# Gated complex recurrence and a maxout feed-forward block on one core: another order of all steps, with fewer changes of the array's tile shape

## The chip, the core and the metric

The kernel runs on one NeuronCore of a Trainium2 chip. The metric is the device time of one execution in microseconds (us). A profiled execution gives a span, which runs from the first to the last recorded instruction; the device time holds some more around it.

## The reference, cut to what matters

```python
# B, H, S, D = 4, 8, 768, 48; all float32
mag = np.sqrt(a_re * a_re + a_im * a_im)
scale = np.minimum(mag, 0.999) / (mag + 1e-06)
a_re_n, a_im_n = (a_re * scale, a_im * scale)
for t in range(S):                      # complex state S_re, S_im of D x D for each batch and head
    ar, ai = (a_re_n[:, :, t, :, None], a_im_n[:, :, t, :, None])
    new_re = ar * S_re - ai * S_im
    new_im = ar * S_im + ai * S_re
    kv = np.einsum('bhd,bhe->bhde', k[:, :, t], v[:, :, t])
    S_re, S_im = (new_re + kv, new_im)
    y[:, :, t] = np.einsum('bhd,bhde->bhe', q[:, :, t], S_re)
x = y.transpose(0, 2, 1, 3).reshape(B * S, H * D)          # 3072 x 384
h = np.maximum(np.maximum(x @ w1, x @ w2), x @ w3)         # weights 384 x 768
out = h @ w_out                                            # 768 x 384
```

The four weights of the feed-forward block lie in DRAM as 64-bit floats; the kernel makes 32-bit floats of them itself.

## The kernel before

The 3072 tokens are worked in 12 groups of two tiles x and y of 128 tokens each (two batches, the same 128 positions). A step is a word such as `Ay:4`: step A of tile y of group 4. A long text, `SCHEDULE`, lists all steps of all groups; the kernel runs through it once and emits the instructions of each step as it comes to it. Nothing reorders them afterwards: each engine's proxy ties every instruction to the one before it on the same engine,

```python
                if self.last is not None:
                    tc.add_manual_dep(ins.ins, self.last.ins.name, order, reason="the schedule's order")
```

so the text fixes the order on TensorE (PE), VectorE (DVE), ScalarE (ACT), GpSimd (POOL) and the DMA queues of SP and POOL. Waits between engines come from the data and from the buffers.

Two more lists go with it. `SLOTS` has one digit for each PSUM tile that a step takes, in order: `tag="ps" + next(slots)`, four rooms 0, 2, 4 and 6 of two banks each, so it says which earlier result has to be read before a step may write. `OTHER` names the steps that run on their second engine (DVE in place of ACT, or DVE in place of an accumulating DMA of POOL; for `Zf`, `Zg` POOL in place of DVE).

The steps, by the names that come back below:

- Weights. Twelve blocks of w1, w2, w3 and w_out. `WL` loads a block raw on SP's queue into a room that is free at that time (a part of the weights' own store, the activations' buffer `xhx`, or `strassen`, the buffer of later sums); `Wb`, `Wc`, `We` (DVE, 128x768 elements) and `Wa` (ACT) convert it. `Wg` adds one block into another by a DMA of POOL (or on DVE). `T`, `t`, `M`, `m` make a product of w1 and w_out, `wp`, used by the first group; `J1` to `J4` make differences of w_out for the later groups.
- Gates. `Lr`, `Li` load a_re and a_im; `sqr`, `sqi`, `add`, `lnL`, `expe`, `expw`, `lne`, `relu`, `Lnop`, `abs`, `addw`, `pw`, `lnw`, `expL`, `mulai`, `mulw`, `stt`, `xor`, `half`, `atan`, `turn` turn them into the logarithm of the magnitude (`Ln`) and the angle (`w`), on ACT and DVE; for group 0 the steps are done for each half alone (`sqr0`, `sqr1` and so on).
- Angles. `cs` (PE) cumulates the angles, `t`, `nf`, `af`, `sa`, `sb` make sine and cosine. `Cd` carries the last angle into the next group by a small DMA of POOL.
- Attention by chunks of 64 positions. `sums` (PE) cumulates `Ln`; `En`, `Ek`, `Eq` are its exponentials; `mk`, `mq`, `uk`, `uq`, `kEn` scale k and q; `tpk`, `tpq` (PE) transpose them, `Kc`, `Qc` bring them to SBUF; `F` (PE) and `f0` to `f3` (ACT) make the decay factors at the boundaries of sub-chunks, `Q1`, `Q2`, `KB`, `QB`, `QG` apply them; `A` and `B` (PE) are the scores, `g0` to `g3` (DVE) and `b0`, `b1` (ACT) pick their valid parts into `atm`; `dk` (PE) and `h0` to `h3` advance the state; `y` (PE) is the output of the tile, the step `x` (`xx`, `xy`) copies it for the feed-forward part.
- Feed-forward. For group 0, tile by tile: `U01x` to `U22y` are the products with w1, w2, w3 (PE), `u..` the maxima (DVE, ACT), `O` the product with w_out, `o` its copy. For groups 1 to 11, with both tiles at once: `U01`, `U02`, `U11`, `U12` and the maxima; then the output product in the seven products `P1` to `P7` of a Strassen scheme (PE, four matmuls each), beside `Px` and `Py`, with the sums `S1` to `S4` ahead of them and `r1`, `r6`, `r75`, `r57`, `ox`, `oy` behind them on DVE (`r1` on ACT). `Dx`, `Dy` store a tile's 192 KB on SP's queue.

The order interleaves the feed-forward products of one group with the attention of the next one and the gates of the one after it.

A matmul's tile shape is the part of the 128x128 array that it uses. `U`, `O`, `P`, `Px`, `Py`, `T`, `M`, `pw` use all rows and columns; `F`, `sums`, `dk` use 64x64 quarters; `A`, `B`, `y` use 32 columns, four of them side by side; `tp` 64 rows, `cs` 64 columns. A stay, below, is a stretch of PE's list that keeps one shape. `A` is 64 small matmuls each with a weight load of its own, `B` 32, `y` 112, `dk` 64, `tp` 32, `F` and `sums` 16 each (each list a little shorter for the first chunk of a sequence), while `U` is 18 large ones, `P` four, `O` nine.

All instructions are recorded under one line, L201, since one helper emits them; they are told apart by the names of their tiles.

Of the kernel before, what the change touches and what calls it, by code (L numbers as in the profile page):

```python
# [26 lines left out]
turn1:0 nfx:0 Wc9:0 afx:0 Wa10:0 T2:0 sqr:1 sqi:1 sax:0 sbx:0 t2:0 Wc10:0 We9:0 add:1 ukx:0 WL11:0 Lvx:0 uqx:0 We10:0
csy:0 tpkx:0 tpqx:0 lnL:1 ty:0 Kcx:0 Eqy:0 expw:1 kEnx:0 xor:1 nfy:0 Lky:0 Liy:2 Lix:2 WL1:0 WL2:0 Lrx:2 WL4:0 Lvy:0
Lry:2 dkx:0 Fy:0 Wb11:0 relu:1 Qcx:0 expe:1 QBx:0 Q2x:0 mqy:0 abs:1 Wa11:0 Wc11:0 Wb1:0 half:1 lne:1 f2y:0 Eny:0 f1y:0
Eky:0 f3y:0 h1x:0 f0y:0 pw:1 Wa1:0 lnw:1 expL:1 We11:0 Wb2:0 Q1x:0 h2x:0 Wc1:0 h3x:0 QGx:0 Wa2:0 afy:0 say:0 mulai:1  # L30
We1:0 CL:0 Wb4:0 Wc2:0 mulw:1 We2:0 M0:0 M1:0 Zg:0 Lnop:1 Cdx:0 Wg1:0 Cdy:0 Wa4:0 sby:0 sqr:2 sqi:2 sumsx:1 Ax:0 M2:0
Wg2:0 stt:1 Wc4:0 mky:0 atan:1 uqy:0 Ekx:1 Eqx:1 Enx:1 We4:0 add:2 lnL:2 expe:2 relu:2 g0x:0 g1x:0 uky:0 KBx:0 g2x:0
g3x:0 turn:1 m1:0 Bx:0 b0x:0 tpqy:0 tpky:0 m0:0 b1x:0 Kcy:0 WL5:0 Lkx:1 csx:1 csy:1 tx:1 yx:0 xor:2 Qcy:0 Wb5:0 nfx:1
Q2y:0 Q1y:0 ty:1 expw:2 afx:1 Wa5:0 xx:0 abs:2 Ay:0 sax:1 QBy:0 Wc5:0 KBy:0 We5:0 addw:2 kEny:0 nfy:1 g0y:0 g1y:0 g2y:0
g3y:0 Wg4:0 Z4:0 Wg5:0 half:2 Cdx:1 Z3:0 WL7:0 WL8:0 Lqx:1 Lqy:1 Lky:1 U11x:0 sumsy:1 dky:0 By:0 lnw:2 Wb7:0 QGy:0
u11x:0 expL:2 mulai:2 mulw:2 Eny:1 Eky:1 Eqy:1 b0y:0 Wa7:0 h1y:0 b1y:0 afy:1 U02x:0 U01x:0 yy:0 u01x:0 xy:0 sbx:1 say:1
sby:1 h2y:0 Wc7:0 Cdy:1 Z2:0 Lvx:1 h3y:0 stt:2 U12x:0 Liy:3 atan:2 lne:2 We7:0 u12x:0 mkx:1 mqx:1 u02x:0 ukx:1 turn:2
mky:1 uqx:1 Wb8:0 U01y:0 U02y:0 U11y:0 u11y:0 u01y:0 U12y:0 Wa8:0 u02y:0 u12y:0 uky:1 csx:2 tx:2 nfx:2 tpkx:1 tpqx:1
tpky:1 Lnop:2 Wc8:0 We8:0 Wg7:0 Kcx:1 Kcy:1 Qcx:1 U21y:0 Fx:1 sumsx:2 Fy:1 Lix:4 f3x:1 f1x:1 f2x:1 f0x:1 f3y:1 f1y:1
f2y:1 f0y:1 u21y:0 csy:2 kEnx:1 Q1x:1 Wg8:0 ty:2 Eqx:2 Ekx:2 U21x:0 u21x:0 Enx:2 mqy:1 uqy:1 Q2x:1 nfy:2 U22y:0 dkx:1  # L40
tpqy:1 Qcy:1 afy:2 say:2 h0x:1 h1x:1 QBx:1 Ax:1 g0x:1 u22y:0 KBx:1 g1x:1 Lqx:2 Lky:2 Lvy:1 Lkx:2 Lix:3 h0y:1 mqx:2 h2x:1
Q2y:1 h3x:1 Q1y:1 g2x:1 g3x:1 sbx:2 sqi:3 sby:2 afx:2 Oy:0 Fx:2 oy:0 sax:2 Bx:1 b1x:1 b0x:1 Ay:1 QGx:1 yx:1 Lvx:2 Lrx:3
Lry:3 Lqy:2 U22x:0 kEny:1 QBy:1 g0y:1 g1y:1 g2y:1 KBy:1 g3y:1 f2x:2 f3x:2 xx:1 sqr:3 sumsy:2 Eqy:2 f0x:2 f1x:2 add:3
u22x:0 dky:1 By:1 Ox:0 J3:0 mkx:2 h1y:1 b1y:1 Eny:2 Eky:2 lnL:3 expe:3 b0y:1 relu:3 h2y:1 ukx:2 mky:2 uqx:2 xor:3 uky:2
QGy:1 expw:3 ox:0 abs:3 tpkx:2 tpqx:2 kEnx:2 h3y:1 yy:1 Kcx:2 Qcx:2 xy:1 dkx:2 Fy:2 addw:3 mqy:2 Q2x:2 half:3 QBx:2
f1y:2 f0y:2 f3y:2 lne:3 lnw:3 expL:3 f2y:2 uqy:2 h0x:2 KBx:2 Q1x:2 U11:1 u11:1 mulw:3 h1x:2 J1:0 Lnop:3 tpky:2 tpqy:2
kEny:2 Ax:2 Kcy:2 Qcy:2 Lrx:4 Lry:4 Lvx:3 Liy:4 Dx:0 Lvy:2 U01:1 Q1y:2 g0x:2 g1x:2 g2x:2 Q2y:2 g3x:2 mulai:3 h2x:2 h3x:2
Cdy:2 Cdx:2 sumsy:3 Bx:2 u01:1 Ay:2 Fx:3 KBy:2 g0y:2 g1y:2 h0y:2 b0x:2 b1x:2 Eny:3 g2y:2 stt:3 Eqy:3 sqr:4 atan:3 g3y:2
U02:1 U12:1 QGx:2 QBy:2 J2:0 turn:3 sqi:4 f1x:3 f0x:3 f2x:3 f3x:3 add:4 yx:2 u12:1 u02:1 csx:3 csy:3 lnL:4 xx:2 tx:3
xor:4 S1:1 nfx:3 dky:2 sumsx:3 ty:3 nfy:3 h1y:2 Eky:3 expe:4 Enx:3 Eqx:3 expw:4 S2:1 QGy:2 h2y:2 h3y:2 relu:4 afx:3 S3:1  # L50
By:2 Ekx:3 P5:1 P6:1 P1:1 P7:1 sax:3 sbx:3 Lqy:3 Lqx:3 abs:4 mqx:3 afy:3 b0y:2 b1y:2 say:3 r1:1 sby:3 addw:4 lne:4 Lix:5
Dy:0 Lry:5 Lkx:3 Lvx:4 Px:1 P2:1 S4:1 mkx:3 P3:1 Py:1 J4:0 yy:2 xy:2 r6:1 r75:1 uqx:3 ukx:3 Lky:3 mqy:3 uqy:3 r57:1
mky:3 tpkx:3 tpqy:3 tpqx:3 Lrx:5 Lvy:3 Liy:5 h0x:3 Kcx:3 kEnx:3 P4:1 Qcy:3 lnw:4 Qcx:3 uky:3 dkx:3 Fy:3 U11:2 f1y:3
expL:4 f0y:3 Lnop:4 oy:1 Q2x:3 half:4 mulai:4 mulw:4 f3y:3 f2y:3 h1x:3 QBx:3 Q1x:3 ox:1 stt:4 h0y:3 sqi:5 h2x:3 Q1y:3
Cdx:3 Cdy:3 h3x:3 Dy:1 Dx:1 atan:4 sqr:5 add:5 lnL:5 turn:4 Lix:6 Lqy:4 Lry:6 Lrx:6 Lky:4 Lqx:4 U01:2 u01:2 u11:2 U02:2
tpky:3 Kcy:3 csy:4 expe:5 ty:4 relu:5 xor:5 u02:2 S3:2 QGx:3 csx:4 tx:4 expw:5 abs:5 Ax:3 nfy:4 nfx:4 KBx:3 kEny:3 g0x:3
g1x:3 afx:4 U12:2 u12:2 g2x:3 g3x:3 S1:2 Fx:4 f2x:4 f3x:4 f1x:4 f0x:4 sumsy:4 Eny:4 Eqy:4 Eky:4 Lkx:4 dky:3 Lvy:4 Liy:6
sumsx:4 Bx:3 Ekx:4 Eqx:4 S2:2 Q2y:3 mqy:4 h1y:3 addw:5 sby:4 sbx:4 sax:4 b1x:3 b0x:3 h0x:4 h2y:3 KBy:3 h3y:3 mky:4 QBy:3
mkx:4 ukx:4 P7:2 P6:2 P5:2 P1:2 yx:3 Ay:3 xx:3 lnw:5 lne:5 expL:5 r1:2 Enx:4 Px:2 Py:2 P4:2 QGy:3 S4:2 r6:2 g0y:3 g1y:3
g2y:3 g3y:3 afy:4 mulw:5 r75:2 half:5 P2:2 By:3 P3:2 b1y:3 b0y:3 yy:3 say:4 xy:3 r57:2 mqx:4 uqx:4 ox:2 mulai:5 tpqx:4  # L60
tpkx:4 oy:2 kEnx:4 Fy:4 uky:4 Lnop:5 Kcx:4 uqy:4 sumsx:5 U11:3 KBx:4 Lqx:5 Cdx:4 f2y:4 stt:5 f3y:4 Ekx:5 f0y:4 Lkx:5
Dy:2 Dx:2 Qcx:4 Enx:5 Q1x:4 Cdy:4 u11:3 Eqx:5 QBx:4 mkx:5 QGx:4 U01:3 atan:5 Q2x:4 u01:3 f1y:4 h0y:4 U02:3 u02:3 sqr:6
dkx:4 h1x:4 sqi:6 h2x:4 h3x:4 Fx:5 f0x:5 f3x:5 add:6 f1x:5 f2x:5 Ax:4 g0x:4 Lqy:5 g1x:4 Bx:4 lnL:6 expe:6 g2x:4 g3x:4
U12:3 lne:6 b1x:4 tpky:4 turn:5 mqx:5 b0x:4 tpqy:4 Qcy:4 u12:3 kEny:4 S1:3 csy:5 ty:5 csx:5 Kcy:4 dky:4 nfy:5 S3:3
sumsy:5 h1y:4 h2y:4 tx:5 nfx:5 h3y:4 afy:5 yx:4 Eky:5 Eny:5 Eqy:5 afx:5 Q2y:4 Q1y:4 sbx:5 P5:3 P1:3 P7:3 Lky:5 sax:5
# [1 line left out]
Py:3 r1:3 By:4 P2:3 P4:3 say:5 sby:5 QGy:4 g1y:4 abs:6 g2y:4 g3y:4 b1y:4 b0y:4 KBx:5 mqy:5 r6:3 r75:3 r57:3 kEnx:5 oy:3
Q1x:5 uky:5 xor:6 Lry:7 sqr:7 Fy:5 f2y:5 sumsx:6 uqy:5 f3y:5 yy:4 P3:3 ox:3 f0y:5 Lkx:6 xy:4 QGx:5 addw:6 U11:4 Liy:7
Dx:3 QBx:5 Ekx:6 mkx:6 Enx:6 Lvx:5 f1y:5 lnw:6 Lqx:6 h0y:5 u11:4 Q2x:5 expL:6 mulai:6 mulw:6 U01:4 u01:4 tpky:5 h0x:5
Eqx:6 Kcy:5 tpqy:5 stt:6 Ax:5 Lix:7 atan:6 g0x:5 Qcy:5 g1x:5 g2x:5 Bx:5 kEny:5 g3x:5 b0x:5 Q2y:5 U02:4 sqi:7 b1x:5 add:7  # L70
lnL:7 relu:7 expe:7 u02:4 U12:4 Fx:6 f2x:6 S3:4 f3x:6 half:6 turn:6 f0x:6 u12:4 Lvy:5 dky:5 h1y:5 Q1y:5 f1x:6 sumsy:6
dkx:5 Eny:6 csy:6 csx:6 h1x:5 mqx:6 S1:4 Dy:3 ty:6 nfy:6 S2:4 Eqy:6 Lqy:6 mqy:6 Eky:6 P1:4 KBy:5 tx:6 nfx:6 afx:6 lne:7
expw:7 afy:6 P7:4 abs:7 Lky:6 Ay:5 QBy:5 g0y:5 g1y:5 g2y:5 yx:5 g3y:5 addw:7 sbx:6 sax:6 ukx:6 uqx:6 By:5 say:6 P5:4
xx:5 P6:4 r1:4 r6:4 lnw:7 xor:7 S4:4 half:7 Px:4 P2:4 b0y:5 Py:4 r75:4 P4:4 r57:4 P3:4 expL:7 mulw:7 QGy:5 oy:4 tpqx:6
tpkx:6 b1y:5 Lnop:7 mky:6 Qcx:6 Q1x:6 ox:4 Liy:8 kEnx:6 yy:5 sumsx:7 xy:5 Cdx:6 Enx:7 Fy:6 f2y:6 f0y:6 f3y:6 mulai:7
f1y:6 Eqx:7 QBx:6 QGx:6 Q2x:6 stt:7 Lqx:7 Ekx:7 Lix:8 U01:5 sqi:8 Lry:8 Cdy:6 Kcx:6 Lrx:8 Lvx:6 dkx:6 h1x:6 sby:6 mqx:7
# [966 lines left out]
```

## Time and profile before

| | |
|---|---|
| device time, median of 3 runs | 558.63 us (558.34 to 559.18) |
| profiled execution, span | 553.2 us, 22687 instructions |
| PE matmuls busy | 523.6 us (95%), x10086 |
| PE weight loads busy | 448.1 us (81%), x10086 |
| DVE busy | 482.1 us (87%), x752 |
| ACT busy | 368.2 us (67%), x653, of which 49 table loads 62.9 us |
| POOL busy | 70.8 us (13%), x113 |
| DMA | 47.51 MB, mean 86 GB/s |

For the profiled execution only the span is listed, no device time of its own; the difference between the median and the span is 5.4 us. PE's busy time counts from the start of a matmul to its modelled end, and weight loads (PEld) run beside it. In the rows of the profile, `A<-Q,K 112*32 112x80` means that tile A is written from Q and K, the stationary tile takes 112 rows and 32 columns of the array, and the moving one is 112x80; `x64` is the number of instructions in the row, and a bracket behind a row gives the idle time of the engine ahead of it and what ended it. "issue" stands for idle time in which the engine waited for nothing that the profile shows. Queue q8 carries instructions that are fetched.

### The profile page before, as it was taken

To read this page: it belongs to the slowest core of one execution; us is meant where nothing else is said; L and a number is where in the kernel's file an instruction comes from. 1 tells how busy PE (TensorE), PEld (TensorE's weight loads), DVE (VectorE), ACT (ScalarE), POOL (GpSimd) and SP (SyncE) were. 2 spreads that over 40 slices of the span, in tenths; PEclk is the share of its full clock that TensorE was granted. 3 is DMA by queue.
4 is the path that set the end of the run, shared out by engine and by line. 5 is a ranking of instruction groups with operands and counts; after the bars stand their busy time and mean duration, and the time that the engine had idled before them with its cause. 6 is when DMAs were issued, how large, how long until landed. Compare 5 with 4: busy or idle time off the path is not lost.

```text
span 553.2 us, 22687 instructions
## 1 busy us (share of the span) xinstructions
PE 523.6 (95%) x10086; PEld 448.1 (81%) x10086; DVE 482.1 (87%) x752; ACT 368.2 (67%) x653; POOL 70.8 (13%) x113
## 2 busy tenths in 40 slices
...
GB/s 203 295 246 176 174 131 79 50 128 63 109 38 124 67 68 51 61 44 88 72 121 58 35 85 108 101 91 54 62 125 20 32 105 72 2 31 2 31 1 28
DMA packets 141953, 47.51 MB, mean 86 GB/s; under 512 B 130464, under 2 KB 135584, under 8 KB 141856
## 3 DMA queue, kind: packets, MB, share of 16 engines
...
q8 instruction: 79, 1.29, 1.0%
q14 instruction: 18, 0.15, 0.1%
...
## 4 chain that ended last, share of the span: by engine, by line
PE 84%; DVE 7%; ACT 4%; SPq 2%; issue 1%; DMA 1%; DVEq 0%; ACTq 0%
PE up L201 33%; PE op L201 24%; PE y L201 7%; PE A L201 5%; PE tp L201 4%; PE dk L201 3%; PE sums L201 2%; PE cs L201 2%; DVE w L201 2%; SPq L201 2%; PE F L201 2%; PE B L201 1%; DMA wo<-in_moe_w_dram 1%; DVE atm L201 1%; ACT f L201 1%
## 5 line engine op out<-in xcount | busy, mean ns | idle before, releaser
L201 PE MATMUL up<-xhx,w 128*128 128x256 f32 x792 | 177.0, 382 | 0.1
L201 PEld LDWEIGHTS up<-xhx,w 128*128 128x128 f32 x792 | 148.6, 190 | 21.5 <-PE B L201 0.3
L201 ACT ACT_TABLE_LOAD x49 | 62.9, 1283 | 1.6 <-PEq L1027 0.8
L201 ACT COPY atm<-B 32x128 f32<-32x128 f32 x96 | 24.6, 256 | 37.8 <-DVE atm L201 19.7
L201 PE MATMUL op<-wo,xhx 128*128 128x192 f32 (+1 forms) x220 | 48.4, 363 | 0.0
L201 DVE TENSOR_TENSOR Q<-Q,f 112x1024 f32<-112x1024 f32 (+1 forms) x48 | 45.4, 952 | 1.7 <-ACT Q L201 1.2
L201 POOL DMA_DIRECT2D ar<-nf x40 | 34.6, 1305 | 60.3 <-DVE ar L201 48.9
L201 ACT ACTIVATE f<-F 48x232 f32<-48x232 f32 x96 | 34.5, 359 | 10.1 <-PE F L201 6.1
L201 PEld LDWEIGHTS op<-wo,xhx 128*128 128x128 f32 x220 | 36.5, 190 | 4.6 <-issue 0.6
L201 PE MATMUL y<-atm,vb 128*32 128x64 f32 x1152 | 39.0, 221 | 0.2 <-ACT K L201 0.2
L201 PE MATMUL y<-QG,g 112*32 112x64 f32 x1408 | 38.0, 219 | 0.2 <-issue 0.2
L201 PEld LDWEIGHTS y<-atm,vb 128*32 128x32 f32 x1152 | 32.4, 109 | 5.3 <-issue 2.9
L201 PEld LDWEIGHTS y<-QG,g 112*32 112x32 f32 x1408 | 34.8, 109 | 0.3 <-issue 0.3
L201 DVE TENSOR_TENSOR ot<-ot,op 128x384 f32<-128x384 f32 (+1 forms) x56 | 25.6, 464 | 10.7 <-PE op L201 6.4
L201 PE MATMUL op<-wo,strassen 128*128 128x192 f32 x176 | 33.0, 331 | 0.0
L201 POOL DMA_DIRECT2D Ln<-e x9 | 8.3, 923 | 192.2 <-ACT e L201 53.8
L201 PE MATMUL A<-Q,K 112*32 112x80 f32 x1536 | 31.6, 234 | 1.4 <-DVE Q L201 1.4
L201 DVE COPY_PREDICATED atm<-masko,A 128x256 f32<-128x256 uint8 x72 | 31.2, 435 | 1.7
L201 PE MATMUL op<-w,strassen 128*128 128x192 f32 x176 | 32.2, 329 | 0.0
L201 PEld LDWEIGHTS A<-Q,K 112*32 112x32 f32 x1536 | 27.3, 110 | 4.2 <-issue 3.1
L201 PEld LDWEIGHTS op<-wo,strassen 128*128 128x128 f32 x176 | 28.8, 190 | 0.8
L201 ACT COPY Q<-tp 112x1024 f32<-112x1024 f32 x22 | 22.3, 1014 | 10.7 <-PE tp L201 10.5
...
## 6 DMA issues: line engine op xcount, KB each, us to landing
ar<-in_a_re_dram SPq DMA_DIRECT2D x24, 192.0 KB, 3.1
ai<-in_a_im_dram SPq DMA_DIRECT2D x24, 192.0 KB, 3.5
...
out_dram<-ot SPq DMA_DIRECT2D x23, 192.0 KB, 2.6
...
```

The source lines that it names most:

```text
L201: ins = f(*a, **kw)
```

## The change

The three lists are replaced: the order of all steps, the PSUM rooms and the choice of engines. The work is the same. PE's list has 167 stays in place of 190. Weight blocks are loaded and converted in another order at the start, and steps of equal or like shape stand together more often: two `U` or all `P` steps in a row, `tpk` beside `tpq`, and `A`, `y`, `B` beside each other. The order of group 4 to 11 around some of the places, old list above and new list below (parts of lines):

```
-Ay:4 xx:4 KBy:4 ukx:5 uqx:5 Lrx:7 tpqx:5 S2:3 expw:6 relu:6 QBy:4 Lnop:6 mky:5 tpkx:5 S4:3 Kcx:5 g0y:4 Qcx:5 P6:3 Px:3
-Py:3 r1:3 By:4 P2:3 P4:3 say:5 sby:5 QGy:4 ...
+expL:6 sbx:5 Q1y:4 h1x:4 P1:3 P7:3 h1y:4 Q2y:4 h2x:4 QBy:4 h3x:4 h2y:4 S1:3 h3y:4 Ay:4 g0y:4 yx:4 By:4 afx:5 g1y:4
+xx:4 sax:5 g2y:4 S2:3 g3y:4 b1y:4 sqr:7 P5:3 Py:3 P4:3 Px:3 P6:3 S4:3 b0y:4 r1:3 QGy:4 mqx:5 mulai:6 mulw:6 uqx:5 r6:3
...
+Lnop:7 tpqx:6 QBy:5 Ay:5 g0y:5 g1y:5 afy:6 g2y:5 Qcx:6 Q1x:6 g3y:5 lnw:7 yx:5 xx:5 By:5 b0y:5 QBx:6 b1y:5 P2:4 QGy:5
...
+Liy:10 h2x:7 h3x:7 lnw:9 r6:6 r75:6 r57:6 b1y:7 QGy:7 xx:7 sumsx:8 dky:7 h1y:7 Fx:8 yy:7 S4:6 Enx:8 Ekx:8 expL:9 h2y:7
...
+dkx:10 h1x:10 dky:10 Fx:11 Ekx:11 h2x:10 h3x:10 f0x:11 f3x:11 f1x:11 f2x:11 afx:11 sumsy:11 Eky:11 Eqy:11 Eny:11
+h1y:10 KBy:10 h2y:10 Ay:10 g0y:10 Lkx:11 Lqx:11 h3y:10 yx:10 By:10 mqy:11 g1y:10 g2y:10 Px:9 P2:9 Lky:11 g3y:10 S1:9
...
-dkx:11 u02:10 S3:10 Ax:11 Dy:9 g0x:11 Q1y:11 h0x:11 h1x:11 h1y:11 U12:10 u12:10 Ay:11 S1:10 g0y:11 g1y:11 g1x:11 Bx:11
+Q1y:11 h1x:11 Q2y:11 QGx:11 KBy:11 U12:10 u11:10 QBy:11 u12:10 S1:10 P1:10 P7:10 Ay:11 yx:11 By:11 g0y:11 S2:10 g1y:11
```

The head and the end:

```
-Lrx:0 sqr0:0 Lix:0 sqi0:0 add0:0 lnL0:0 expe0:0 expw0:0 lne0:0 relu0:0 WL0:0 Wb0:0 Liy:0 Wa0:0 sqi1:0 Zf:0 Lry:0 sqr1:0
-WL3:0 Lqy:0 Lry:1 WL6:0 WL9:0 Lkx:0 Lix:1 WL10:0 Lqx:0 Lrx:1 Liy:1 Lnop0:0 abs0:0 Fx:0 pw0:0 sumsx:0 add1:0 xor0:0
+Lix:0 sqi0:0 Lrx:0 xor0:0 Zf:0 sqr0:0 add0:0 CL:0 Zg:0 Liy:0 sqi1:0 lnL0:0 expe0:0 expw0:0 lne0:0 relu0:0 Lry:0 sqr1:0
+xor1:0 Lnop0:0 add1:0 abs0:0 pw0:0 WL0:0 Wb0:0 lnL1:0 sumsx:0 half0:0 expe1:0 expw1:0 relu1:0 lne1:0 Lnop1:0 WL3:0
...
+dkx:0 h1x:0 afx:1 Ekx:1 QBx:0 Wc4:0 half:2 We4:0 Wg4:0 Ay:0 Bx:0 b1x:0 b0x:0 yx:0 Lkx:1 Eqx:1 g0y:0 Enx:1 lnw:2 h2x:0
...
+h1y:0 b0y:0 WL7:0 Wc5:0 U01x:0 u01x:0 stt:2 U11x:0 atan:2 Lky:1 Wb7:0 yy:0 xy:0 h2y:0 We5:0 turn:2 Z2:0 Wa7:0 sby:1
...
-u01:11 U11:11 U02:11 u11:11 u12:11 P1:11 S3:11 Dy:10 u02:11 S1:11 S2:11 Px:11 P2:11 P5:11 S4:11 P6:11 r1:11 r6:11 Py:11
-P3:11 P7:11 r75:11 ox:11 P4:11 Dx:11 r57:11 oy:11 Dy:11
+u02:11 U11:11 U12:11 u11:11 u12:11 Px:11 P3:10 S1:11 S3:11 P6:10 Dy:9 r6:10 P5:11 P7:11 r75:10 S2:11 P6:11 Py:11 P4:11
+P1:11 r57:10 S4:11 P3:11 oy:10 ox:10 Dx:10 r1:11 Dy:10 r6:11 r75:11 r57:11 P2:11 ox:11 Dx:11 oy:11 Dy:11
```

Three small edits of the code go with the lists: step `t` of the angles and step `r1` may run on DVE where `OTHER` names them, and `P2` and `P3` may come in either order.

```diff
-            activation(out=T["t", x], in_=T["cs", x], func=AF.Copy, scale=-1.0, bias=MAGIC)
+            if other():
+                dve.tensor_scalar(out=T["t", x], in0=T["cs", x], scalar1=-1.0, scalar2=MAGIC, op0=OP.mult, op1=OP.add)
+            else:
+                activation(out=T["t", x], in_=T["cs", x], func=AF.Copy, scale=-1.0, bias=MAGIC)
...
+            last = i not in (2, 3) or ("half", g) in T
+            if i in (2, 3):
+                T["half", g] = i
             for n in range(4):
                 mm(out=r[i], lhsT=left[:, n], rhs=factor(i)[:, (n + 2 * (g % 2)) % 4],
-                   start=i in (1, 5, 6, 7) and n == 0, stop=i != 2 and n == 3)
+                   start=i in (1, 5, 6, 7) and n == 0, stop=last and n == 3)
...
             if name == "r1":
-                act.copy(out=xl, in_=r[1])
+                copy(out=xl, in_=r[1])
```

The new `OTHER` names `tx:5`, `ty:5`, `ty:9`, `ty:10` and `r1:1`, `r1:4` among its steps.

More of the change, by code (lines that the diff above doesn't have):

```diff
@@ L27 @@
[L27 to L65, printed above, removed]
-Ay:4 xx:4 KBy:4 ukx:5 uqx:5 Lrx:7 tpqx:5 S2:3 expw:6 relu:6 QBy:4 Lnop:6 mky:5 tpkx:5 S4:3 Kcx:5 g0y:4 Qcx:5 P6:3 Px:3
@@ L67 @@
[L67 to L76, printed above, removed]
```

143 lines of the change are left out of this document (93 added, 50 removed).

## The prediction

> **What bounds the kernel now.** I read the page's first lines, then a table of busy time by stretch, the chain of waits, and last the time line of PE's weight loads. The page says that PE is the fullest engine and heads the chain that ended last; its 20172 records of matmuls and weight loads come to the 1.29 MB that queue q8 fetched, at 64 bytes each, in 79 blocks.
>
> ```profile
> span 553.2 us, 22687 instructions
> PE 523.6 (95%) x10086; PEld 448.1 (81%) x10086; DVE 482.1 (87%) x752; ACT 368.2 (67%) x653; POOL 70.8 (13%) x113
> q8 instruction: 79, 1.29, 1.0%
> PE 84%; DVE 7%; ACT 4%; SPq 2%; issue 1%; DMA 1%; DVEq 0%; ACTq 0%
> 0.00:20.00 20.00, 9.33 (x75) 4.81 (x76) 11.92 (x26) 16.04 (x35) 15.01 (x49) 1.00 0.92 239
> 20.00:91.70 71.70, 58.28 (x1110) 46.40 (x1112) 70.75 (x113) 65.99 (x111) 16.56 (x17) 0.95 0.80 178
> 91.70:140.00 48.30, 47.99 (x1096) 38.15 (x1087) 46.84 (x72) 35.88 (x65) 4.22 (x5) 1.00 0.42 82
> 140.00:549.60 409.60, 408.01 (x7824) 358.79 (x7818) 351.93 (x543) 250.28 (x444) 35.07 (x42) 1.00 0.32 63
> ```
>
> The columns of the stretches are length, then busy time of PE, PEld, DVE, ACT, POOL. Two regimes are to be seen. Up to 91.7 us, where PE starts step O of the first tile, DVE is busy 82.7 us: 8.1 us of its idle time lie in the first 20 us, 1.0 behind them. PE idles 24.1 us there. So DVE's list, converting weights beside the first attention tiles, sets when PE gets to that place. From 91.7 on PE is busy 456.0 of 457.9 us, and the end is PE's remaining work. Busy PE is not PE at its pace, so gaps inside its steps have to be looked for separately.
>
> The span is 553.2 us and the runs' median 558.63; 5.4 us lie outside the span, and I carry that over.
>
> **The price of a change of shape.** A stay of PE in one shape costs a fixed amount beside its matmuls, which shows where two equal steps stand together instead of apart (pieces of the chain: start, length, step, records):
>
> ```profile
> 122.76 4.08 PE up L201 x18
> 129.68 7.97 PE up L201 x36
> 385.59 1.50 PE op L201 x8
> 399.74 2.80 PE op L201 x16
> 396.90 1.04 PE tp L201 x32
> 485.65 1.93 PE tp L201 x64
> 397.94 0.81 PE sums L201 x16
> 449.45 1.46 PE sums L201 x32
> 98.52 0.46 PE L201 MATMUL B<-QB,KB 112*32 112x32 f32 x32
> 98.80 1.33 PE L201 MATMUL A<-Q,K 112*32 112x80 f32 x64
> 341.88 0.46 PE L201 MATMUL B<-QB,KB 112*32 112x32 f32 x32
> 342.27 1.14 PE L201 MATMUL dk<-vb,uk 64*64 64x48 f32 x64
> ```
>
> Twice 4.08 less 7.97 is 0.19 us for a stay in the full shape (0.20 from op), 0.15 for tp, 0.16 for the 64x64 steps. For the 32-column steps A, B and y, B hands over after 0.28 us to its own shape and after 0.39 to another: 0.11, and I take 0.13 with an allowance for the way in, which no row parts. [...]
>
> Counted on the two lists, 190 stays become 167. Behind step O 156 become 140: 9 fewer of 32 columns, 4 of 64x64, 4 of tp, one more of the full array. That is 9 x 0.13 + 4 x 0.16 + 4 x 0.15 - 0.19 = **-2.2 us** (-1.9 to -2.6). The 7 fewer ahead of it fall where PE waits for DVE, and count nothing.
>
> **DVE's list up to step O.** Taking each instruction at the pace of its group, it holds 83.3 us against 83.4: no difference. The added choices (t and r1 may go to DVE: 4 and 2 times, about 0.5 us each) are paid for by others of the step list going back to ACT, and ACT's two more table loads come behind step O, where ACT is idle 172 of the 457.9 us of the last two stretches. **0.**
>
> **The head.** DVE's idle time of the first 20 us decides, since nothing gives it back before step O:
>
> ```profile
> 5.45 0.56 DVE L201 CUSTOM_DVE_ANT_0 L<-L,e 128x384 f32<-128x384 f32 x1 [2.50 <-ACT L L201]
> 8.20 0.87 DVE L201 TENSOR_SCALAR xhx<-w 128x768 f32<-128x768 f32 x1 [2.19 <-DMA w<-in_moe_w_dram]
> 10.80 0.56 DVE L201 CUSTOM_DVE_ANT_0 L<-L,e 128x384 f32<-128x384 f32 x1 [1.14 <-ACT e L201]
> 14.30 0.61 DVE L201 SCALAR_TENSOR_TENSOR Ln<-L,e 128x384 f32<-128x384 f32 x1
> 17.05 0.63 DVE L201 TENSOR_SCALAR xhx<-wo 128x768 f32<-128x768 f32 x1 [1.01 <-DMA wo<-in_moe_w_dram]
> ```
>
> The new list loads the four 192 KB pieces of a ahead of weight block 0, which moves from third to fifth. At the 239 GB/s of the first stretch its 0.77 MB then end about 1.6 us later than the 8.2 us of this row. Lnop0 stays at about 9.0; the second half's chain of five ACT steps (0.42 us apart) brings Lnop1 to about 12.6 instead of 14.3, but with only Wb0 and half0 to fill the time DVE idles some 1.6 us before it, then 0.7 at mqx (it waits for PE's cold sums), and 0.3 twice. My hand chain puts DVE's idle time at 9.1 to 9.6 against 8.1 to 8.7: **+1.0 us** (0 to +2).
>
> **The tail.** PE now waits 1.2 us before its last step, P4, for DVE's ox, and DVE then has 0.6 us to do:
>
> ```profile
> 548.01 1.57 PE L201 MATMUL op<-w,xhx 128*128 128x192 f32 x8 [1.23 <-DVE ot L201]
> 549.61 0.62 DVE L201 TENSOR_TENSOR ot<-ot,op 128x192 f32<-128x192 f32 x2 [1.40 <-PE op L201]
> out_dram<-ot SPq DMA_DIRECT2D x23, 192.0 KB, 2.6
> ```
>
> In the new list the last step is P2, and on the built program it has no wait on DVE; ox then comes behind it, 0.46 us by its pace. With the gap seen in PE's starts (1.4 us) that is **-0.9 us** (-1.4 to 0). What could be late next is r1, which must wait for the store Dx of the group before; between P6 of that group and P1 PE has 7 us of steps, and the chain of DVE steps and the store (3.3 + 2.6 us by its median) fits.
>
> **The instruction fetches.** This is the term that decides. Inside steps, with no wait in the program, PE stops:
>
> ```profile
> 100.21 0.11 PEld L201 LDWEIGHTS y<-atm,vb 128*32 128x32 f32 x1
> 100.67 0.11 PEld L201 LDWEIGHTS y<-QG,g 112*32 112x32 f32 x1 [0.35 <-issue]
> 104.79 0.33 PEld L201 LDWEIGHTS dk<-vb,uk 64*48 64x48 f32 x18 [0.25 <-issue]
> 100.66:104.78 4.12, 3.99 (x128) 3.60 (x127) 4.05 (x9) 2.86 (x6) 0.00 (x0) 1.00 0.51 92
> 196.56 0.33 PEld L201 LDWEIGHTS y<-atm,vb 128*32 128x32 f32 x3
> 196.79 0.11 PEld L201 LDWEIGHTS y<-QG,g 112*32 112x32 f32 x1
> q8 instruction: 1, 0.02, 5.2%
> q8 instruction: 1, 0.02, 5.5%
> ```
>
> Between the two stops lie 128 matmuls and 127 loads: one block of 256 instructions with the semaphore step among them. The q8 rows are those of 98.2 to 99.4 us and of 101.7 to 103.4; times 16 engines and the length of the stretch, the one fetch took 1.0 us and the next 1.5; between 99.4 and 101.7 none ran. So PE went on 1.4 us after the first fetch had ended and 1.5 after the second, and asked for the second 1.1 us after it had entered a block. A third stop shows at 196.6: three loads that start within some 0.03 us elsewhere in that step are spread over 0.33. By the starts of the matmuls and the ends of the q8 packets none of the 79 blocks is entered sooner than 1.4 us behind the end of its fetch. My reading: one block is fetched ahead, asked for when the block before it is entered, and 1.1 + 1.0 + 1.4 = **3.5 us** pass at least between entries of the sequencer, which runs up to some 50 instructions ahead of the array.
>
> How fast can PE eat a block? Steps of small tiles are rich in instructions:
>
> ```profile
> 505.83 1.24 PE A L201 x64
> 518.91 1.72 PE y L201 x112
> ```
>
> A is 128 instructions (64 matmuls, 64 loads) in 1.24 us, y 224 in 1.72: a block of these lasts 1.8 to 2.0 us, while one U (36 instructions) lasts 3.9. A block that lies wholly inside such steps, with its predecessor's end there too, costs up to 1.7 us; one that begins behind a U or a P costs nothing, since the sequencer has run ahead.
>
> Counting instructions on the list of before, semaphore steps included, from the phase that the stops give (192 past a multiple of 256), every block behind 100 us passes this rule with nothing or at most 0.2 us. On the new list, at the same phase, these blocks break it (the time it takes; the lead of the sequencer; what is left of 3.46):
> - Ay, yx, By of group 4: 1.81, 0.42, 1.2
> - Ay, yx, By of group 5: 1.74, 0.39, 1.3
> - By, yx of group 7, sumsx of 8, dky of 7: 2.38, 0.27, 0.8; and at once dky:7, Fx:8, yy:7: 1.85, none, 1.6
> - dkx, dky of group 10, Fx, sumsy of 11: 2.09, 0.33, 1.0; and at once Ay, yx of group 10: 2.13, none, 1.3
> - Ay, yx of group 11: 1.90, 0.42, 1.1
>
> Together 8.4 us, all behind 140 us, where PE has 1.6 us of idle time to hide them. With 3.3 us as the least distance it is 7.2, with a lead of a hundred instructions 4, with 3.7 us 10.5. One more of 1.3 us, at Ay:0, lies in the part that DVE sets and counts nothing. Before's own 0.3 us behind 140 go. **+8.1 us** (4 to 10.5).
>
> **The sum.** -2.2 + 0 + 1.0 - 0.9 + 8.1 = +6.0: span 559.2, time **564.6**.
>
> **Rivals.**
> *The fetches don't bind* (faster). Nearly all of the 79 blocks pass without a stop; if several blocks were held ahead, a run of 400 small instructions would pass too, and the stops of the trace would have another cause. Then -2.2 + 1.0 - 0.9 = -2.1 is left: 556.5 (555 to 557.5 with the head's 0 to 2). Against it: the stops stand a whole block apart, each 1.4 to 1.5 us behind a fetch's end, and the fetch starts only when a block is entered. Chance 0.18. [...]
> *They bind half* (same). The sequencer leads by more than the 50 instructions that I take, and about 2 us of stops meet the 2.1 us saved: 557.5 to 559.7, 0.05.
> *Both, and a weight block late* (slower still). Block 7 may load only when We4 has freed its room; on DVE's list that is 51.8 us, its first use Wb7 60.7: 8.9 us, where before left 17.3. A block into the same room, asked for at 34.25, was used first at 44.78:
>
> ```profile
> 34.25 1.02 SPq L201 DMA_DIRECT2D strassen<-in_moe_w_dram x1
> 44.78 0.56 DVE L201 TENSOR_SCALAR xhx<-strassen 128x768 f32<-128x768 f32 x1
> ```
>
> So it had landed after 10.5 us at the latest. Past 8.9 each microsecond moves step O by as much: up to 1.6, and up to 3 if the new list puts more in the queue before it, 566 to 569. Against it: 10.5 is an upper end, and DMA is busy 0.80 in this stretch. 0.09.
> The forecast itself, 560 to 568, has 0.68.
>
> **How the numbers follow.** A measurement here tells 0.2% (1.1 us) from no change. Faster 0.18; same 0.05; slower 0.68 + 0.09 = 0.77. The range leaves out the faster case and the thin ends: 559.4 (stops of 4 us, head at 0) to 568.5 (stops of 10.5, head at +2).
>
> **What would show it.** PEld rows with "issue" of 0.8 to 1.6 us inside y, B, dk, sums and A at the places listed, each 1.4 us behind the end of a q8 packet, with PE's chain 84% or more; the up and op rows unchanged in mean; DVE idle some 9 us in the first 20. I am wrong if those rows are missing, if a block of A and y passes in 2 us, or if the time is under 558; the head is wrong if DVE's idle time up to step O is not 9.5 to 11 us.

## The result, and the profile after

The changed kernel takes 573.99 us (median of 4 runs, 571.01 to 576.3) against 558.9 us before (558.34 to 559.28): a ratio of 1.0277, interval 1.0239 to 1.0316. It is slower, as forecast, but by 15.1 us where 6.0 were forecast, and lies outside the range. The profiled execution took 574.46 us with a span of 572.8.

The page of the changed kernel, its size, PE's line and the shares of the chain:

```profile
span 572.8 us, 22687 instructions
PE 526.3 (92%) x10086; PEld 452.1 (79%) x10086; DVE 477.6 (83%) x750; ACT 373.3 (65%) x657; POOL 70.8 (12%) x113
PE 80%; DVE 7%; issue 5%; DMA 3%; ACT 3%; SPq 2%; DVEq 0%; ACTq 0%; POOLq 0%
```

"issue" went from 1% of the chain to 5%: its pieces come to 30.6 us in place of 7.6, of which one of 3.9 at 143 us stands ahead of a transfer of POOL and is no stop of PE. The table by stretch (length, busy time of PE, PEld, DVE, ACT, POOL, then PE's granted clock), cut at step O of the first tile, which now starts at 97.8 us in place of 92.0:

```profile
0.00:20.00 20.00, 8.04 (x80) 3.96 (x82) 13.68 (x31) 17.05 (x36) 14.79 (x49) 1.00 0.95 236
20.00:97.80 77.80, 61.16 (x1116) 48.70 (x1116) 67.87 (x106) 66.03 (x116) 17.68 (x19) 0.85 0.81 178
97.80:140.00 42.20, 41.54 (x810) 32.90 (x808) 40.41 (x62) 29.63 (x49) 5.30 (x6) 1.00 0.51 97
140.00:568.80 428.80, 415.61 (x8086) 366.54 (x8084) 354.94 (x552) 260.62 (x459) 33.06 (x39) 0.99 0.30 57
```

The span grew by 19.6 us: 5.8 ahead of step O, 13.8 behind it. That is more than the 15.1 us between the medians, since the profile of before shows a faster execution than its listed runs (see the point on span and time below). DVE idles 6.3 us of the first 20, less than the 8.1 of before; it loses its time later, 9.9 us between 20 and 97.8. PE's stops stand in PEld's rows (start, length, operation, records, and in brackets the idle time ahead and "issue"). The first two lie ahead of step O, the others behind it. Counted in records of the trace, a step F is 32 matmuls, P eight and O 18, twice what the list of steps above gives.

```profile
61.39 0.28 PEld L202 LDWEIGHTS A<-Q,K 112*32 112x32 f32 x11 [3.15 <-issue]
69.47 0.51 PEld L202 LDWEIGHTS B<-QB,KB 112*32 112x32 f32 x29 [3.79 <-issue]
110.68 0.25 PEld L202 LDWEIGHTS dk<-vb,uk 64*64 64x64 f32 x11 [0.79 <-issue]
193.60 0.12 PEld L202 LDWEIGHTS y<-atm,vb 128*32 128x32 f32 x4 [3.19 <-issue]
236.45 0.25 PEld L202 LDWEIGHTS B<-QB,KB 112*32 112x32 f32 x20 [1.19 <-issue]
285.99 0.17 PEld L202 LDWEIGHTS B<-QB,KB 112*32 112x32 f32 x9 [1.72 <-issue]
364.96 0.27 PEld L202 LDWEIGHTS dk<-vb,uk 64*48 64x48 f32 x13 [1.85 <-issue]
368.57 0.23 PEld L202 LDWEIGHTS y<-QG,g 112*32 112x32 f32 x8 [1.07 <-issue]
460.07 0.31 PEld L202 LDWEIGHTS F<-cuts,Ln 64*48 64x48 f32 x19 [0.70 <-issue]
487.58 0.19 PEld L202 LDWEIGHTS sums<-Ln,rest 64*64 64x64 f32 x3 [1.65 <-issue]
491.33 0.11 PEld L202 LDWEIGHTS y<-QG,g 112*32 112x32 f32 x1 [1.23 <-issue]
531.86 0.11 PEld L202 LDWEIGHTS y<-atm,vb 128*32 128x32 f32 x1 [0.81 <-issue]
```

Every one stands at the beginning of a block of 256 instructions, counted as in the prediction, and 1.2 to 1.6 us behind the end of a q8 packet. Seven of them are those that were listed: By:4, By:5, dky:7, yy:7, sumsy:11, yx:10 and yx:11, together 9.5 us for the 8.4 of the list. Three more (dky:1, yx:3, Fy:10) bring 4.7, and the two in the head 6.9.

What ran ahead of the long unlisted ones is seen in the DMA queues (q0 carries POOL's transfers, q1 SP's loads; kind: packets, MB, share of 16 engines) of two stretches, each followed by the short one in which the fetch ran; 60 to 67 us and 67 to 68.2, then 188.2 to 191.2 and 191.2 to 192.3:

```profile
q0 software_dynamic: 597, 0.69, 58.4%
q1 hardware_dynamic: 1302, 0.95, 49.8%
...
q8 instruction: 1, 0.02, 5.0%
...
q0 software_dynamic: 174, 0.39, 72.7%
q1 hardware_dynamic: 620, 0.11, 22.8%
...
q8 instruction: 1, 0.02, 5.1%
```

The block of 61.39 was entered at that time; its successor's fetch started only at 67.1, 5.7 us later, while the loads and POOL's accumulating transfers held the DMA engines full. Ahead of yx:3 it was some 3.1 us, ahead of Ay:0 4.6 us (q0 has 46.5% there), both counted from where the block begins. Behind seven of the stops no other packet ran, and the next fetch started 1.05 to 1.18 us after the block was entered. The fetch itself took 0.9 to 1.0 us in the three long cases.

Full engines alone do not explain this. In the profile of before the fetch behind 100.67 us started after 1.12 us, although SP's loads took 0.98 of the engines' time until then; with 24 small matmuls ahead (the next section) the one behind 122.61 us started after 1.22, at 1.06. The three long cases of this trace have POOL's queue in common. What decides how long a fetch waits stays open.

### The profile page after: what moved, and what is told of

It is laid out like the page before. It is cut to its first block, busy times and chain, and to the rows that moved or that the text cites. A ratio compares the mean times of both kernels' runs of the same rounds, so it can differ in the third digit from the quotient of the medians.

```text
span 572.8 us, 22687 instructions
## 1 busy us (share of the span) xinstructions
PE 526.3 (92%) x10086; PEld 452.1 (79%) x10086; DVE 477.6 (83%) x750; ACT 373.3 (65%) x657; POOL 70.8 (12%) x113
## 4 chain that ended last, share of the span: by engine, by line
PE 80%; DVE 7%; issue 5%; DMA 3%; ACT 3%; SPq 2%; DVEq 0%; ACTq 0%; POOLq 0%
PE up L202 32%; PE op L202 20%; PE y L202 6%; PE A L202 5%; PE tp L202 4%; PE dk L202 4%; PE sums L202 2%; DVE w L202 2%; PE cs L202 2%; SPq L202 2%; PE F L202 2%; PE B L202 1%; DMA w<-w 1%; DVE xhx L202 1%; ACT L L202 1%
## 5 line engine op out<-in xcount | busy, mean ns | idle before, releaser
L202 PE MATMUL op<-wo,xhx 128*128 128x192 f32 (+1 forms) x220 | 50.8, 370 | 0.0
L202 POOL DMA_DIRECT2D ar<-nf x40 | 34.6, 1350 | 98.1 <-DMA vb<-in_v_dram 49.0
L202 PE MATMUL y<-atm,vb 128*32 128x64 f32 x1152 | 41.5, 228 | 5.0 <-issue 3.7
L202 DVE TENSOR_TENSOR Q<-Q,f 112x512 f32<-112x512 f32 (+1 forms) x48 | 45.0, 949 | 0.1
L202 PE MATMUL y<-QG,g 112*32 112x64 f32 x1408 | 40.7, 225 | 2.0 <-issue 2.0
L202 PEld LDWEIGHTS y<-atm,vb 128*32 128x32 f32 x1152 | 34.8, 114 | 8.5 <-issue 7.4
L202 PEld LDWEIGHTS y<-QG,g 112*32 112x32 f32 x1408 | 37.0, 113 | 2.3 <-issue 2.3
L202 ACT COPY ot<-op 128x192 f32<-128x192 f32 (+1 forms) x11 | 3.8, 344 | 48.5 <-PE op L202 48.5
L202 DVE TENSOR_TENSOR xhx<-xhx,up 128x768 f32<-128x768 f32 x22 | 20.9, 951 | 12.6 <-PE up L202 12.0
L202 ACT ACTIVATE xhx<-up 128x768 f32<-128x768 f32 x17 | 13.8, 810 | 25.6 <-PE up L202 25.5
```

The lines of the kernel that those rows point to most:

```text
L202: ins = f(*a, **kw)
```

## The experiments

**The phase alone.** The order of before, moved within its blocks by small matmuls at the start, where PE has nothing to do:

```diff
+    spare = ones("spare", 32)
+    cold = psum.tile([P, 2, 512], FP, tag="ps6", name="cold")
+    for _ in range(24):          # or 64, or 4
+        mm(out=cold[0:32, 0, 0:4], lhsT=spare, rhs=spare[:, 0:4], start=True, stop=True)
     program(SCHEDULE, 0)
```

> The kernel before with 24 small matmuls into a spare PSUM room at the very start, while PE waits for its first input: 48 records of matmuls and 48 of weight loads more, so every later instruction lies 96 places further in its block of 256. The order of all steps, the shapes and the waits stay. Fetch theory: by the rule of the prediction (3.46 us at least between entries of blocks, a lead of 48 instructions) the blocks of this phase lose 17 us, where those of before lose none, and more where the DMA queues are full: 575 us (568 to 585). Rivals: if the time of the changed kernel comes from waits between engines in its order, or from a lower granted clock on its own, nothing changes here: 558.9 us, at most 0.3 more.

Measured: 580.87 us, 1.0416 of before (1.0375 to 1.0458; before 556.28 on that chip).

> The same with 64 small matmuls at the start: 256 instructions more, one whole block, so that all later instructions lie in their blocks as before. Fetch theory: no stops but those of before, 559 us (558.3 to 559.8), although 40 more matmuls run than with 24. If the extra matmuls themselves cost time (head, clock), it is slower than the kernel with 24.

Measured: 558.61 us, ratio 1.0019 (0.9989 to 1.005). What PE waited for behind 91 us, with 24 matmuls (first rows: total, times, longest), and below it the only row with 64:

```profile
PE F L201 <- issue: 4.8, 4, 1.9
PE y L201 <- issue: 4.6, 4, 2.0
PE B L201 <- issue: 4.6, 4, 1.5
PE dk L201 <- issue: 2.5, 3, 1.4
PE A L201 <- issue: 2.2, 3, 1.0
...
PE sums L201 <- issue: 0.6, 1, 0.6
PE tp L201 <- issue: 0.4, 1, 0.4
```

```profile
PE op L201 <- DVE ot L201: 1.2, 1, 1.2
```

19.7 us of stops, 20 of them, each at the first or second instruction of a block, out of nothing but 96 instructions at the start; with 256, a whole block, they are gone. So the fetch is the cause of this loss, and not the waits of the order: the order, the shapes and the data are the same in both. It also shows that the order of before holds only at its own place in the blocks. The changed order was not run at another place, so how it would do there is not known.

> The kernel before with 4 small matmuls at the start, 16 instructions. Fetch theory: by the rule this phase has no stop either, and the small ones of before (0.40, 0.33, 0.22 and 0.1 us) change by at most as much: 0.5 us faster, between 0.9 faster and 0.3 slower. Rivals: no change.

Measured: 558.38 us, 1.0025 of before (1.0002 to 1.0048). Missed: this phase is slightly worse, where 0.5 us less was expected. Its trace has stops of 0.5 us at yx:1, 0.3 at sumsy:2 and 0.2 at yy:3 and dky:8, hardly more than the small ones of before. What its profile lost lies ahead of step O, which starts at 94.8 us; the two kernels with another tail (below), on the same chip, have 92.6 and, with the same 4 matmuls, 92.5. So where the loss comes from is not shown.

**The fetch by itself.** The loop of a kernel of its own, with and without transfers beside it:

```python
for src, nm in ((a_re, "ar"), (a_im, "ai"), (q, "q"), (k, "k")):      # 96 loads of 192 KB
    ...
for n in range(20):                                                  # 192 matmuls each
    small(192, "A%d" % (n % 2))
```

> A kernel of its own: 3840 small matmuls (weight tile 112x32, moving 112x64, as in y) in one row, 15360 instructions, with no wait between them; for about the first 70 us 96 loads of 192 KB run on SP's queue beside them; the output is written as zeros and nothing of the reference is computed. Fetch theory: behind the loads a block of 256 instructions takes 3.4 to 3.6 us although PE's own pace (y: 224 instructions in 1.72 us) would be 2.0; beside the loads it takes longer, 4 to 7 us, because the fetch waits among the loads' packets. Rival: 2.0 us per block in both stretches, or the same in both if the loads don't matter.

The table by stretch (PE, PEld, DVE, POOL, clock, DMA share, GB/s), beside the loads and behind them:

```profile
12.00:112.00 100.00, 60.49 (x2875) 56.64 (x2868) 0.00 (x0) 0.00 (x0) 0.78 0.85 166
140.00:240.00 100.00, 55.74 (x3508) 51.42 (x3500) 0.00 (x0) 0.00 (x0) 0.98 0.02 4
```

Behind the loads 7008 instructions in 100 us, 3.65 us for 256, though PE is busy only 56% of the time; beside them 5743, 4.46 us. So the floor is there with all but empty queues (DMA share 0.02), a little above the 3.46 that the prediction took. The 0.8 us more are not the queues' alone, since the clock is lower there, 0.78 against 0.98. In the pieces of the trace with a clock of 1.00 a block takes 4.1 us beside the loads and 3.6 behind them, so the queues add 0.5 on average. The loads lasted to 128 us and not to 70; in their last piece, 114.8 to 121.6 us with 366 GB/s and the clock at 1.00, one block took 7.2 us. For a run of small matmuls these rows thus show 3.65 us from block to block, where PE's own pace in step y of before (224 instructions in 1.72 us) would give 2.0.

**The changed kernel with its runs of small steps broken.** Pairs of P steps moved (parts of lines):

```diff
-P1:3 P7:3 h1y:4 Q2y:4 h2x:4 QBy:4 h3x:4 h2y:4 S1:3 h3y:4 Ay:4 g0y:4 yx:4 By:4
+P1:3 h1y:4 Q2y:4 h2x:4 QBy:4 h3x:4 h2y:4 S1:3 h3y:4 Ay:4 g0y:4 yx:4 P7:3 P5:3 By:4
...
-yx:5 xx:5 By:5 b0y:5 QBx:6 b1y:5 P2:4 QGy:5
+yx:5 xx:5 P3:4 P2:4 By:5 b0y:5 QBx:6 b1y:5 QGy:5
...
-P1:6 P5:6 P6:6 QBy:7 r1:6 g0y:7 g1y:7 g2y:7 g3y:7 Cdy:8 Cdx:8 By:7 b0y:7 yx:7
+P1:6 QBy:7 r1:6 g0y:7 g1y:7 g2y:7 g3y:7 Cdy:8 Cdx:8 By:7 b0y:7 P5:6 P6:6 yx:7
...
-P1:10 P7:10 Ay:11 yx:11 By:11 g0y:11 S2:10 g1y:11 g2y:11 P5:10
+P1:10 Ay:11 P7:10 P5:10 yx:11 By:11 g0y:11 S2:10 g1y:11 g2y:11
```

> The changed kernel with four pairs of its own P steps (1.57 us a pair) moved into runs of small steps: P7, P5 of group 3 ahead of By:4; P3, P2 of group 4 ahead of By:5; P5, P6 of group 6 ahead of yx:7; P7, P5 of group 10 ahead of yx:11. Nothing else moves. Four more stays in the full shape and four more of 32 columns: by the price of shapes alone 1.3 us slower. Fetch theory: the stops at By:4 (1.28), By:5 (1.80), dky:7 (1.93) and yx:11 (0.91) shrink by up to 1.57 each, 5.3 together, so 4 us faster than the changed kernel (2 to 7), and the trace shows them gone or under 0.4 us. Rivals (waits of the order, clock): the stops stay, 1 us slower.

Measured: 569.18 us, 1.0215 of before (1.0168 to 1.0262). The stops at By:4 and yx:11 are gone, that at By:5 is 0.2, that at dky:7 fell from 1.85 to 0.85, and that at yy:7 grew from 1.07 to 1.34. The rows of B of tile y:4:

```profile
233.59 0.35 PEld L202 LDWEIGHTS B<-QB,KB 112*32 112x32 f32 x32 [0.23 <-issue]
```

From U12:3 to P2:11 the two traces differ by 4.4 us (345.1 us, now 340.7), as expected, although the edit adds eight stays. That the sum came out so close is in part luck: the stops in this stretch fell by 5.3 us, from 10.2 to 4.9; a stretch of lower clock at group 7, some 2.4 us in the changed kernel (see the granted clock below), is missing here; and PE's waits for DVE and ACT grew by 2.0. The rest of the 8.8 us between the two spans is not the edit's: 1.1 lies ahead of step O, and 2.6 is a stop at yx:3 of 0.6 us in place of 3.2, the cause of which is not shown. This profile is the fastest of the kernel's four executions (565.68 us); by the two ratios to before, 1.0215 and 1.0277, it gains some 3.4 us on the changed kernel, and their intervals overlap, so it is the trace that shows the effect.

**The head.** First two, then four accumulations moved from POOL's DMA to DVE:

```diff
-Zf:0 Zg:0 relu:1 Kcx:0
+Zf:0 Zg:0 addw:2 Wg4:0 relu:1 Kcx:0
```

> The changed kernel with steps addw:2 and Wg4:0 on DVE in place of the accumulating DMAs of POOL (two transfers of 384 KB less between 56 and 69 us, two DVE steps of some 0.9 us more). Fetch theory with the full queues: the two fetches there that started 4.6 and 5.7 us after their blocks were entered start sooner, the stops inside Ay:0 and By:0 (3.2 and 3.9 us) shrink by 1 to 2.5 each, and step Oy:0 starts 1 to 3 us sooner than at 97.8 although DVE has 1.9 us more to do; the later stops stay. Rival: the stops in the head are waits of another kind, or DVE's list sets Oy:0 as the prediction had it: the stops stay at 3 us or more, and Oy:0 comes 1 to 2 us later.

Measured: 570.4 us, 1.0240 of before (1.0203 to 1.0277); Oy:0 at 96.8. PE's waits from 50 to 98 us:

```profile
PE up L202 <- DMA w<-w: 3.4, 1, 3.4
PE dk L202 <- issue: 2.6, 1, 2.6
PE A L202 <- issue: 1.4, 1, 1.4
...
PE B L202 <- issue: 0.6, 1, 0.6
```

In this view the two stops were 3.0 and 3.7 us long; they shrank by 1.6 and 3.1. The row of 2.6 at dkx:0 is no fetch: it does not stand at the beginning of a block, and it ends 0.06 us behind DVE's step nf, as a wait of 0.7 does at the same place of the changed kernel, so it is a wait for DVE's longer list. Another wait grew too, from 1.0 to 3.4 us, that for POOL's transfer which adds one weight block to another. The fetch behind the first stop still started 2.9 us after the block was entered, although POOL's queue took only 0.01 of the engines' time there, so its transfers are not all of the delay. A gain in the head is not shown: the kernel with the moved pairs, whose head is that of the changed kernel, has Oy:0 at 96.7.

> The changed kernel with the four moved pairs of P steps and with four accumulations on DVE in place of POOL's DMA: addw:2, Wg4:0, Wg5:0, Wg7:0. Fetch theory with full queues: the stops in the head are those of the kernel with two accumulations moved or less, and the wait of 3.4 us for the DMA that adds one weight block to another is gone, so Oy:0 starts at 93 to 95 us in place of 96.8 and 97.8; behind it the moved pairs bring 4 us as before: 565 us (562 to 568). Rival: DVE's list, now 3.7 us longer than in the changed kernel, sets Oy:0, which stays at 97 or later, and the time at 569 or more.

Measured: 569.48 us, 1.0221 of before (1.0154 to 1.0287); Oy:0 at 98.1. Missed: the wait for the weight block is gone, but PE waits 2.0 us for ACT's xhx in the head instead, and step O comes no sooner. Both figures of the rival came in; that DVE's 3.7 us of added work are the reason fits, but is not shown. So a test was needed that leaves DVE, ACT and the DMAs alone; B is changed in the same way as A, and 8 small matmuls stand at the start:

```diff
-            for h in range(H):
+            for h in range(H if x < C else 0):
+                mm(out=ps[:, h // HU, h % HU * P:h % HU * P + 80], lhsT=T["K", x][0:DD, h],
+                   rhs=T["Q", x][0:DD, 4 * h], start=True, stop=True)
+            for h in range(0 if x < C else H):
                 for o in range(0, P, 32):
...
```

> The changed kernel with A and B of group 0 (Ax, Ay, Bx, By) as one matmul over all 128 columns in place of four of 32 columns: 72 matmuls fewer, and 8 small ones at the start in return, so 256 instructions (one block) less and all later blocks as in the changed kernel. Three quarters of these scores are computed from the wrong part of Q, so the output of the first group is wrong. DVE, ACT and all DMAs keep their lists. Fetch theory: with one block less between sumsy:1 and dky:0 one of the two stops of 3.2 and 3.9 us goes or both shrink, DVE and ACT wait less for PE there, and Oy:0 starts 2 to 4 us sooner than at 97.8; the time falls by as much, to 571 us (569 to 573) on a chip where the changed kernel takes 574. Rival: the waits in the head come from DVE's or ACT's lists or from weights that land late; Oy:0 stays within 1 us of 97.8.

Measured: 569.52 us, 1.0232 of before (1.0192 to 1.0271). PE's waits from 50 to 98 us, all of them, and the chain at step O:

```profile
PE up L202 <- DMA w<-w: 1.9, 1, 1.9
PE y L202 <- ACT atm L202: 1.2, 1, 1.2
PE dk L202 <- DVE nf L202: 0.7, 1, 0.7
PE A L202 <- DVE atm L202: 0.4, 1, 0.4
PE sums L202 <- DVE nf L202: 0.2, 1, 0.2
```

```profile
94.69 5.81 PE op L202 x18
```

No stop is left there and Oy:0 starts at 94.5, 3.3 us sooner than in the changed kernel and 2.2 sooner than in the one with the moved pairs, which has the same head. PE's own work did not shrink: Ay takes 2.0 us in this form and 1.24 in the other. So 2.2 to 3.3 of the 5.8 us lost in the head come from the fetches. For the rest there are two candidates, neither of them tested: the wait of 1.9 us for the added weight block, the largest row that before lacks, and the granted clock, 0.50 from 62.6 to 69.5 us here and 1.00 in before from 36.2 us on.

**The price of a shape.** In a kernel of its own, the same matmuls (full array by 192 columns, 112x32 by 64) with 80 or with 40 changes of shape in a part:

```python
for part in range(4):
    k = 1 + part % 2
    for n in range(40 // k):
        large(4 * k, "U%d" % part)
        small(8 * k, "A%d" % (part % 2))
```

> A kernel of its own, in four parts with the same matmuls in each: 160 full-array ones (128x192) and 320 of 32 columns (112x32 by 64), in the first and third part alternating after 4 and 8, in the second and fourth after 8 and 16. A part has 80 changes of shape or 40. The output is zeros, nothing of the reference is computed. By the prices of the prediction (0.19 for a stay in the full shape, 0.13 for one of 32 columns) the second and fourth part are 40 x 0.16 = 6.4 us shorter than the others (5 to 8). Rival: if the price were that of a late fetch, the parts are equal, since instructions and their pace are the same.

Its third and fourth part, by stretch:

```profile
149.10:223.40 74.30, 74.30 (x972) 61.66 (x960) 0.00 (x0) 0.00 (x0) 1.00 0.01 2
223.40:291.20 67.80, 67.80 (x972) 61.30 (x961) 0.00 (x0) 0.00 (x0) 1.00 0.01 2
```

6.5 us for 40 changes, 0.163 us each; 0.16 was expected. (The first part, 77.1, begins with the kernel's start.)

**The tail.** The kernel before, with ox behind P4:

```diff
-P3:11 P7:11 r75:11 ox:11 P4:11 Dx:11 r57:11 oy:11 Dy:11
+P3:11 P7:11 r75:11 P4:11 r57:11 ox:11 Dx:11 oy:11 Dy:11
```

> The kernel before with its last steps in the manner of the new list: r57, ox and Dx behind P4 in place of ahead of it (P3 P7 r75 P4 r57 ox Dx oy Dy). PE's wait of 1.2 to 1.4 us ahead of P4 goes, ox (0.46 us) and the store Dx come behind it: 0.8 us faster than before (0.3 to 1.2), all of it behind 546 us. If the store of Dx then delays that of Dy, no gain.

Measured: 555.59 us, 0.9978 of before (0.9959 to 0.9997; before 556.56 on that chip, its executions from 554.63 to 560.37), so some 1.2 us faster than before, where 0.8 was expected. P7, P4 and DVE's last steps:

```profile
547.50 1.46 PE L201 MATMUL op<-w,strassen 128*128 128x192 f32 x8
548.80 1.46 PE L201 MATMUL op<-w,xhx 128*128 128x192 f32 x8
550.30 1.08 DVE L201 TENSOR_TENSOR ot<-ot,op 128x384 f32<-128x384 f32 x3 [0.36 <-PE op L201]
```

P4 follows P7 with no wait; from P7 to the end it is 7.1 us in place of 7.9. In this execution PE made a stop that the profile of before does not have, 1.48 us at yx:7, with transfers beside it (q1 took 63.1% of the engines' time from 342 to 347.4 us). The order up to there is the same: one execution lost 1.48 us at this place, the other none.

```profile
347.30 0.12 PEld L201 LDWEIGHTS y<-QG,g 112*32 112x32 f32 x4 [1.48 <-issue]
```

> Both edits: the sum of the two, 1.3 us faster than before (0.3 to 2.1).

Measured: 558.78 us, 1.0027 of before (1.0004 to 1.0051). Missed: the two edits don't add up to a gain. Against the tail alone (555.59) the 16 instructions cost 3.2 us; of that the profile shows stops of 0.7 us at yx:1, U02:1 and yy:3.

## Why the prediction was right or wrong, point by point

- **Fewer stays, -2.2 us:** right by what could be measured: 0.163 us for a change between the full array and 32 columns, the one pair that was measured apart. In the changed kernel itself it lies beneath the stops.
- **DVE's list, 0:** right in its busy time up to step O (81.6 us, 82.7 before). That it alone sets step O was wrong: in the changed kernel PE's stops came ahead of it.
- **The head, +1.0 (0 to 2):** wrong in both parts. DVE's idle time of the first 20 us fell to 6.3, where 9.1 to 9.6 were forecast; up to step O it is 16.2, where 9.5 to 11 were. And the stop at Ay:0, priced at 1.3 us and counted as nothing, became two of 3.15 and 3.79; ACT and DVE wait in order behind PE there, and the chain goes through both and then through the weight block:

```profile
59.55 2.68 issue
65.81 3.65 issue
80.02 6.56 DMA w<-w
97.97 5.83 PE op L202 x18
```

- **The tail, -0.9:** right in kind. P2 follows without a wait, and from the last P to the end of the span it is 5.9 us in place of 5.2; with the 1.4 us saved, -0.7.
- **The fetches, +8.1 (4 to 10.5):** the mechanism and seven places were right, the sum was too small: 14.2 us behind step O. The step that failed is the constant: "1.1 + 1.0 + 1.4 = 3.5 us pass at least between entries". As a least distance it held (3.4 us is the shortest of the kernel of small matmuls); as the price of every block it did not. The lead of some 50 instructions can be read in the profile of before: 1.1 us ahead of a fetch's start PE stood, at 49 of the 79 fetches, 0 to 53 records ahead of the first of a block, semaphore steps counted. The 1.1 us came back behind seven stops (1.05 to 1.18), but grew to some 3.1, 4.6 and 5.7 ahead of yx:3, Ay:0 and By:0, and these places were not on the list, or priced too low. They cost 3.19, 3.15 and 3.79 us. The chance that a fetch starts late among other transfers had no term; why it did at these places and not at others with full engines stays open. Of the two blocks of group 7 the first was priced at 0.8 and took 1.85, the second at 1.6 and took 1.07. One reading was off as well: 128 instructions of A in 1.24 us are 2.5 us for a block, not 1.8 to 2.0. The upper end of the range, added up from its terms, is 568.0 and not 568.5.
- **What was not in the sum:** the granted clock. The trace gives 0.50 from 62.5 to 72.7 us in the head and again from 366.3 to 373.1 (the first three rows give means of stretches that overlap these in part). The second one begins 1.3 us behind the end of the first stop of group 7 and ahead of the second. Px of group 6 took 2.76 us in it, where 1.45 is usual (at 151.1 us, at full clock):

```profile
60.00:70.00 10.00, 3.69 (x156) 3.45 (x155) 7.23 (x14) 4.58 (x10) 5.26 (x6) 0.62 0.90 189
360.00:371.40 11.40, 8.74 (x371) 7.74 (x370) 8.76 (x16) 9.51 (x20) 0.00 (x0) 0.77 0.21 39
371.40:373.40 2.00, 2.00 (x6) 1.17 (x4) 2.00 (x4) 1.98 (x3) 0.00 (x0) 0.58 0.00 0
370.64 2.76 PE L202 MATMUL op<-wo,xhx 128*128 128x384 f32 x4
```

  With the 71 matmuls of yy:7 behind the second stop (2.14 us, 1.09 at the usual 1.72 for 112) that is some 2.4 us, an estimate. So the 13.8 us behind step O come out as 14.2 for the stops, less 0.6 for the two that before shows in the prediction's rows, plus 2.4 for the clock, less 2.2 for the stays and 0.7 for the tail: 13.1.
- **From span to time:** 5.4 us was carried over as lying outside the span. In the executions that have both it is 1.7 us (574.46 and 572.8) and, with 64 matmuls at the start, 2.0 (555.32 and 553.3). By that the profile of before took some 555 us, less than any of its listed runs. So the forecast span was 13.6 us short, and the time only 9.4: the difference is luck. Of the 13.6, 4.8 lie in the head, 5.8 in the fetches behind step O and 2.4 in the clock.
- **The rivals:** that the fetches don't bind is refuted by the kernels with 24 and 64 matmuls, and for the changed kernel by the place of its stops and by the moved pairs. A late weight block did appear, but it was the addition of a block by POOL's DMA, and not the load of block 7.
